# Seven products for eight in the last twelve f-tiles, and down tiles summed in DRAM

## The chip, the cores and the metric

The kernel runs on one core of a Trainium2 chip. A core has a matrix engine (TensorE, PE in the profile, with its weight loads shown apart as PEld), VectorE (DVE), ScalarE (ACT), GpSimd (POOL) and SyncE (SP), which here only issues DMAs. Each engine takes its instructions in the order in which they are written; between engines there are semaphores. The metric is the device time of one execution in microseconds, the median of several runs.

## What is computed

One layer norm of x (2048 tokens of 576) feeds two branches, whose results are added to x.

```
xn = layernorm(x)                                   # 2048 x 576
A:  q, k, v = xn @ wqkv;  32 heads of 18; each token attends to 8 earlier ones, 2 apart
    a = softmax(q.k / sqrt(18)) @ v;   A = a @ wo
B:  h  = gelu(layernorm(xn) @ w1);  quarters of h shifted by +1, -1, +2, -2 tokens
    x1 = xn + h @ w2
    B  = x1 + gelu(layernorm(x1) @ w3) @ w4          # w3: 576 x 4608, w4: 4608 x 576
out = x + A + B
```

All inputs and the output are 32-bit floats. The last line of B, the channel MLP with its up projection (w3) and its down projection (w4), is most of the work.

## The kernel before, in words

Products are computed with each operand split into a high part, which the matrix engine takes in its fast 32-bit format, and a low part, the rest. A product of 576 terms is 14 matmuls (`PAIRS`): high by high, high by low and low by high for four slices of 128 rows, and two for the last 64 rows, where high and low share a slice. A low part costs a copy on ACT (the high part) and a subtraction on DVE (`split_w`, L167 and L168, for weights, `split_x` for inputs).

The stages follow each other: q, k and v for 16 tiles of 128 tokens, spilled to DRAM (to about 195 us); the mixing MLP with w1 and w2 (to about 315 us); the channel MLP; the output projection with wo. The channel MLP runs in 72 units. A unit (`for u, (c, b) in enumerate(units)`) takes a pair of f-tiles, of 128 columns of w3 each, and one block of 512 tokens. Its order is:

- two up tiles (`up`, matmuls at L676): 14 matmuls of 512 columns each, gelu twice on ACT (L680 for the high part, L681 in full), the low part on DVE (L682);
- the four down tiles of the unit before (`down`, L696): 12 matmuls of 288 columns each into a PSUM buffer, then an addition to the running sum in `Y` on DVE (L699);
- a share of the weights: loads of w3 and w4 for later f-tiles on SP, their splits on ACT and DVE.

`Y` holds the sums of all 16 token tiles in SBUF for the whole stage. The token blocks come from `n_turn`: the normalised x1 is transposed on DVE, put to DRAM and fetched back in the other layout (`put`, `get`).

The attention (`attention`, a generator) runs on DVE in the gaps of the units: `bg(us)` lets it issue instructions for so many us between two pieces of a unit, by set costs (1.3 us for an operation of 1152 columns). `RATE` sets the amount per unit, 6.1 us. Its eight groups of four heads load q, k and v from DRAM and store their result in `od` (L614). Before the sixth unit from the end, `while not state["done"]` issues whatever is left. Then `load_o`, `o_turn` and `put` bring the attention's result into the layout that the output projection needs: 16 token tiles, loaded by SP (L738), transposed on DVE, put to DRAM by SP (L137) and fetched back. All loads and stores are issued by SP, in the written order; where one waits, those behind it wait.

Of the kernel before, what the change touches and what calls it, by code (L numbers as in the profile page):

```python
# [19 lines left out]
HD = 18  # L20
# [12 lines left out]


# [3 lines left out]
PAIRS += [(4, 4), (4, 9)]  # L38

# [6 lines left out]
def fused_block(ctx, tc, x, wqkv, wo, w1, w2, w3, w4, out):  # L46
# [8 lines left out]
    psa = ctx.enter_context(tc.tile_pool(name="psa", bufs=2, space=PSUM))  # L55
    psb = ctx.enter_context(tc.tile_pool(name="psb", bufs=3, space=PSUM))
# [10 lines left out]
    ST = RT = None  # L67
    xd = {}
    qkvd = dram.tile([24, HALO + S, GC], F32, name="qkvd")
    od = dram.tile([S, D], F32, name="od")  # L70
    bncnt = [0]
# [50 lines left out]
    def room(p):  # L122
        nonlocal ST, RT
        ST = p.tile([128, 20, 128], F32, name="st")
        RT = p.tile([128, 512], F32R, name="rt")
# [19 lines left out]
    def split_x(xt, part=None):  # L145
        raw = xt.bitcast(F32)
        if part != 1:
            act.copy(RT[64:128, :], raw[64:128, 4, :])
            act.copy(xt[0:64, 4, :], raw[0:64, 4, :])
            dve.tensor_tensor(xt[64:128, 4, :], raw[64:128, 4, :], RT[64:128, :].bitcast(F32),  # L150
                              op=ALU.subtract)
# [61 lines left out]
    def ring_block(key):  # L213
        if key not in xring:
            xring[key] = ring.tile([128, 9, 512], F32R, name="xt", tag="xt")
        return xring[key]
# [34 lines left out]
    pool.memset(low, 1.0)  # L251
    for g in range(4):
# [156 lines left out]
    rzp = tc.tile_pool(name="rzp", bufs=2, reuse_waits="tile")  # L409
    rzpool = rzp.__enter__()  # L410
# [3 lines left out]
    def load_w2(k):  # L414
        r = rzpool.tile([128, D], F32, name="rz", tag="rz")
# [80 lines left out]
    raws, W3, W4 = {}, {}, {}  # L496

    def load_f(f):
        if f >= NF:
            return  # L500
        r = raws[f] = wp.tile([128, 640 + D], F32, name="rawf", bufs=2)
        r3 = r[:, :640].rearrange("p (k c) -> p k c", k=5)
        main_rows(r3[:, 0:4, :], w3, f * 128, 128)
        dup_tail(r3[:, 4, :], w3, f * 128, 128)
        sp.dma_start(r[:, 640:], w4[f * 128:(f + 1) * 128, :])

    def split_w3(f):
        if f >= NF:
            return
        t = W3[f] = wp.tile([128, 10, 128], F32R, name="W3", bufs=3)  # L510
        split_w(t[:, 0:5, :], t[:, 5:10, :], raws[f][:, :640].rearrange("p (k c) -> p k c", k=5))

    def split_w4(f):
        if f >= NF:
            return
        t = W4[f] = wp.tile([128, 2, D], F32R, name="W4", bufs=3)
        split_w(t[:, 0, :], t[:, 1, :], raws[f][:, 640:])

    x1n = {}

    def n_turn(t, zpool):
        z = zpool.tile([128, D], F32, name="rz", tag="rz")
        act.activation(z, Y[:, t, :], AF.Identity, bias=RS[2][:, t, 0:1], scale=RS[2][:, t, 1:2])  # L523
        turn(z, t % 4)
        if t % 4 == 3:
            put(("n", t // 4))

    load_f(0)
    load_f(1)
    nsp = tc.tile_pool(name="nsp", bufs=1, reuse_waits="tile")  # L530
    room(nsp.__enter__())
    for t in range(NT):
# [12 lines left out]
        stats(Y[:, t, :], 2, t)  # L545
        if t in (1, 3):
            f = (t - 1) // 2
            split_w3(f)
            split_w4(f)
            load_f(f + 2)  # L550
        if 2 <= t < 6:
            n_turn(t - 2, rzpool)
        if t in (9, 10, 13, 14):
            k = {9: 4, 10: 6, 13: 8, 14: 10}[t]
            n_turn(k, rzpool)
            n_turn(k + 1, rzpool)
        if t in (8, 13):
            x1n[t // 13] = ring_block(("n", t // 13))
            get(("n", t // 13), x1n[t // 13])
        if t in (11, 15):  # L560
            split_x(x1n[t // 15])
    nsp.__exit__(None, None, None)
    rzp.__exit__(None, None, None)
    mp.__exit__(None, None, None)


    xp = ctx.enter_context(tc.tile_pool(name="xp", bufs=1, side="right", reuse_waits="tile"))
    for b in (2, 3):
        x1n[b] = xp.tile([128, 9, 512], F32R, name=f"x1n{b}")
    hp = ctx.enter_context(tc.tile_pool(name="hp", bufs=2, reuse_waits="tile"))  # L570
    tp = ctx.enter_context(tc.tile_pool(name="tp", bufs=1, reuse_waits="tile"))
    room(tp)
# [312 lines left out]
```

## Time and profile before

| | |
|---|---|
| median of 3 runs | 1294.08 us (1294.03 to 1295.88) |
| the profiled execution | 1294.73 us, span 1292.9 us |
| PE busy | 1285.0 us, 99% |
| DVE, ACT, POOL busy | 935.6, 362.0, 38.1 us |
| DMA | 125.20 MB, mean 97 GB/s |

The span is the profiled execution from its first to its last instruction; the time has some 2 us more around it. In the rows of instructions, the columns are line, engine, operation, output and inputs, shapes and count, then the busy time in us and the mean of one in ns. In timelines they are start, duration, engine, line and operation. In the rows by stretch each engine's busy time is followed by its number of instructions, and at the end stand the granted clock of PE, the busy share of the DMA engines and GB/s. In rows of DMAs the last number is the median time from issue to landing in us.

### The profile page before, as it was taken

To read this page: it belongs to the slowest core of one execution; us is meant where nothing else is said; L and a number is where in the kernel's file an instruction comes from. 1 tells how busy PE (TensorE), PEld (TensorE's weight loads), DVE (VectorE), ACT (ScalarE), POOL (GpSimd) and SP (SyncE) were. 2 spreads that over 40 slices of the span, in tenths; PEclk is the share of its full clock that TensorE was granted. 3 is DMA by queue.
4 is the path that set the end of the run, shared out by engine and by line. 5 is a ranking of instruction groups with operands and counts; after the bars stand their busy time and mean duration, and the time that the engine had idled before them with its cause. 6 is when DMAs were issued, how large, how long until landed. Compare 5 with 4: busy or idle time off the path is not lost.

```text
span 1292.9 us, 18505 instructions
## 1 busy us (share of the span) xinstructions
PE 1285.0 (99%) x7678; PEld 1184.8 (92%) x7678; DVE 935.6 (72%) x1336; ACT 362.0 (28%) x601; POOL 38.1 (3%) x108
## 2 busy tenths in 40 slices
PE   8999999999999999999999999999999999999998
PEld 8999998899899999989999999999998999999998
DVE  6455534689576778888878888878888878855741
ACT  3332126524412232232222132232232231213310
POOL 2011100021000000000000000000000000000000
PEclk9999999999999999999999999999999999999999
DMA  7646884346702030221221221221232111156842
GB/s 204 154 122 137 172 174 143 92 108 155 229 29 73 29 101 20 82 75 46 82 73 48 82 72 42 89 73 29 75 99 71 31 49 44 58 120 158 208 145 83
DMA packets 157828, 125.20 MB, mean 97 GB/s; under 512 B 72608, under 2 KB 129824, under 8 KB 157744
## 3 DMA queue, kind: packets, MB, share of 16 engines
q1 hardware_dynamic: 157744, 124.02, 34.9%
q8 instruction: 60, 0.98, 0.3%
q14 instruction: 24, 0.20, 0.0%
HBM read 83.56 MB, written 39.39 MB: 95 GB/s over the span
## 4 chain that ended last, share of the span: by engine, by line
PE 94%; DMA 2%; DVE 2%; ACT 1%; SPq 0%; issue 0%; ACTq 0%
PE ps L696 35%; PE p L676 34%; PE ps L182 17%; PE ps L431 4%; PE ps L276 3%; DMA xd<-st 1%; PE ps L446 1%; PE ps L104 1%; DMA xt<-xd 0%; DMA raw<-in_A_wqkv_dram 0%; DMA x1n<-xd 0%; DVE st L129 0%; SPq L137 0%; PE p L853 0%; ACT rz L523 0%
## 5 line engine op out<-in xcount | busy, mean ns | idle before, releaser
L696 PE MATMUL ps<-W,hi 128*128 128x288 f32 x2304 | 398.7, 294 | 0.5 <-DVE Y L699 0.4
L696 PEld LDWEIGHTS ps<-W,hi 128*128 128x128 f32 x2304 | 339.5, 188 | 7.2 <-DVE Y L699 1.0
L680 ACT ACTIVATE hi<-p 128x512 fp32r<-128x512 f32 x144 | 86.2, 598 | 578.4 <-PE p L676 578.4
L696 PE MATMUL ps<-W,lo 128*128 128x288 f32 x1152 | 245.3, 294 | 0.0
L676 PE MATMUL p<-x1n,W 128*128 128x512 f32 x1008 | 234.6, 389 | 0.0
L676 PE MATMUL p<-xt,W 128*128 128x512 f32 x1008 | 234.4, 389 | 0.0
L676 PEld LDWEIGHTS p<-xt,W 128*128 128x128 f32 x1008 | 187.3, 188 | 36.9
L676 PEld LDWEIGHTS p<-x1n,W 128*128 128x128 f32 x1008 | 187.3, 188 | 36.8
L699 DVE TENSOR_TENSOR Y<-ps,Y 128x576 f32<-128x576 f32 x288 | 212.0, 748 | 11.0 <-PE ps L696 10.7
L682 DVE TENSOR_TENSOR lo<-g,hi 128x512 fp32r<-128x512 f32 x144 | 99.5, 691 | 159.5 <-ACT g L681 159.4
L696 PEld LDWEIGHTS ps<-W,lo 128*128 128x128 f32 x1152 | 185.3, 187 | 0.0
L182 PE MATMUL ps<-WQ,xt 128*128 128x432 f32 x672 | 134.4, 359 | 0.0
L182 PEld LDWEIGHTS ps<-WQ,xt 128*128 128x128 f32 x672 | 125.5, 188 | 5.4
L628 DVE TENSOR_TENSOR prod<-q,k 128x1152 f32<-128x1152 f32 x64 | 86.4, 1349 | 0.0
L631 DVE TENSOR_REDUCE L<-prod 128x64 f32<-128x1152 f32 x64 | 86.1, 1346 | 0.0
L681 ACT ACTIVATE g<-p 128x512 f32<-128x512 f32 x144 | 85.3, 592 | 0.0
L612 DVE TENSOR_TENSOR o<-o,prod 128x1152 f32<-128x1152 f32 x56 | 75.5, 1349 | 0.0
L608 DVE TENSOR_TENSOR prod<-v,L 128x1152 f32<-128x1152 f32 x56 | 75.5, 1348 | 0.0
L167 ACT CAST W<-rawf 128x640 fp32r<-128x640 f32 x72 | 50.3, 700 | 70.5 <-PE ps L696 69.2
L168 DVE TENSOR_TENSOR W<-rawf,W 128x640 fp32r<-128x640 f32 x72 | 56.2, 783 | 0.0
L182 PE MATMUL ps<-W,h 128*128 128x288 f32 x384 | 53.5, 295 | 0.0
L182 PEld LDWEIGHTS ps<-W,h 128*128 128x128 f32 x384 | 51.9, 188 | 0.1
(108 smaller groups left out, 888.7 us busy)
## 6 DMA issues: line engine op xcount, KB each, us to landing
xd<-st SPq DMA_DIRECT2D x48, 320.0 KB, 6.0
qkvd<-stg SPq DMA_DIRECT2D x24, 432.0 KB, 3.6
rawf<-in_B_w_dram SPq DMA_DIRECT2D x36, 288.0 KB, 3.2
rawf<-in_B_w_dram SPq DMA_DIRECT2D x36, 256.0 KB, 3.0
xt<-xd SPq DMA_DIRECT2D x8, 768.0 KB, 5.1
xin<-in_A_x_dram SPq DMA_DIRECT2D x16, 288.0 KB, 3.8
q<-qkvd SPq DMA_DIRECT2D x8, 576.0 KB, 4.0
k<-qkvd SPq DMA_DIRECT2D x8, 576.0 KB, 5.0
```

Source lines behind the costliest of these rows:

```text
L168: dve.tensor_tensor(dst_lo, raw, dst_hi.bitcast(F32), op=ALU.subtract)
L182: pe.matmul(ps[:, h, :n], xs(a), ws(b, h), start=i == 0, stop=i == len(PAIRS) - 1)
L608: dve.tensor_tensor(dst, vv, Lf[:, :, w:w + 1].to_broadcast([128, TPP * GH, HD]), op=ALU.mult)
L612: dve.tensor_tensor(o, o, dst, op=ALU.add)
L628: dve.tensor_tensor(prod.rearrange("p (j h) d -> p j (h d)", h=GH), q, k[:, r0:r0 + TPP, :], op=ALU.mult)
L631: dve.tensor_reduce(Lf[:, :, w], prod, axis=AX.X, op=ALU.add)
L676: pe.matmul(ps, W3[f][:, w, :], x1n[b][:, a, :], start=n == 0, stop=n == len(PAIRS) - 1)
L680: act.activation(by_token(hi), in_order(ps), AF.Gelu_apprx_tanh)
L681: act.activation(by_token(g32), in_order(ps), AF.Gelu_apprx_tanh)
L682: dve.tensor_tensor(lo, g32, hi.bitcast(F32), op=ALU.subtract)
L696: pe.matmul(ps[:, k, :HF], h[:, col], w[:, p, k * HF:(k + 1) * HF], start=n == 0, stop=n == len(seq) - 1)
L699: dve.tensor_tensor(yv, ps[:, :, :HF], yv, op=ALU.add)
```

## The change

The first 12 pairs of f-tiles keep their units, 48 of them. The last 6 pairs (12 f-tiles) run in 12 steps `q`, six for the first 1024 tokens and six for the rest. A step multiplies a 2 x 2 scheme of blocks: the two halves of the 576 terms (288 each), the two f-tiles of the pair, and two blocks of 512 tokens. Instead of eight products of half length it forms seven, of sums and differences of the halves of w3 and of x1 (the scheme of Strassen and Winograd). A product of 288 terms is 7 matmuls (`HALVES`): six for two slices of 128 rows, and one for the last 32 rows, whose high and low parts share a slice.

- The sums of x1's halves are made in DRAM during the units, by accumulating DMAs from POOL (`sums`), and are fetched and split for the first 1024 tokens at the end of the units and for the others in step 5 (`get_op`, `split_op`; `swap`). Signs are put into the blocks when they are made (`n_turn`, `split_n`, `signed`).
- The sums of w3's halves are made in each step for the next one: `load_pair` fetches four blocks with 20 DMAs on SP, `combine` forms the sums on DVE, `split_a` and `split_s` make high and low parts on ACT and DVE.
- The products are added up on DVE (`z_add`) in four temporary tiles, and gelu is taken from these (`gelu_z`).
- Down tiles of 11 of the 16 token tiles (`YD`) are no longer added to `Y` by DVE: ACT copies the PSUM buffer to one of three temporary tiles, and POOL issues a DMA that adds it to a tile in DRAM (`yd`). 198 of the 288 down tiles go this way. At the end SP loads the eleven tiles back (`load_y`). The space of these tiles in `Y` serves as temporary storage and takes the raw w4.
- `RATE` becomes 8.0 us for a unit, 2.0 for the last two, 5.0 for a step, and 0.5 for steps 0, 5 and 6. What is left of the attention is issued before step 8 (`z == -4`). Behind it come `load_o`, `o_turn` and `put`, now one token tile at a time with two buffers, six in steps 8 and 9 each and four in step 10.

The PSUM buffers of the steps are four of 512 columns for products and two for down tiles. The new parts, cut:

```diff
+    def down(t, parts, pd):
...
+        if t in YD:
+            e = temp(EV[evc[0] % len(EV)], D)
+            evc[0] += 1
+            act.copy(e.rearrange("p (h c) -> p h c", h=2), ps[:, :, :HF])
+            pool.dma_start(yd[t], e, accum_op=ALU.add)
+        else:
             yv = Y[:, t, :].rearrange("p (h c) -> p h c", h=2)
             dve.tensor_tensor(yv, ps[:, :, :HF], yv, op=ALU.add)
...
+    def load_pair(q):
+        f = 2 * (NPL + q % NWP)
+        st = WS["st"] = wspool.tile([128, 4, 3, 128], F32, name="w3st")
+        for o, (g, k) in enumerate(((f, 0), (f, 1), (f + 1, 1), (f + 1, 0))):
+            r0, c0 = k * HF, g * 128
+            sp.dma_start(st[:, o, 1:3, :],
+                         w3[r0:r0 + 256, c0:c0 + 128].rearrange("(k p) c -> p k c", p=128))
+            for a in range(4):
+                sp.dma_start(st[32 * a:32 * a + 32, o, 0, :], w3[r0 + 256:r0 + HF, c0:c0 + 128])
...
+    def product(w, xk):
+        ps = pc.tile([128, 512], F32, name="cc", tag="c")
+        for i, (a, v) in enumerate(HALVES):
+            pe.matmul(ps, w[:, v, :], area[xk][:, a, :], start=i == 0, stop=i == len(HALVES) - 1)
+        return ps
...
+    def o_turn(t):
+        turn(otile[t], t % 4)
+        if t % 4 == 3:
+            put(("o", t // 4))
+        if t + 2 < NT:
+            load_o(t + 2)
...
+    ORDER = ["P1", "P2", "P6", "P5", "P7", "D0", "P4", "D1", "P3", "D2", "D3", "D4", "D5", "D6", "D7"]
+    for q in range(NQ):
...
+        if z == -4:
             while not state["done"]:
                 bg(1e9)
             open_wo()
+            for t in range(2):
+                load_o(t)
+        load_w4(p)
...
+        if z < -1:
+            load_pair(q + 1)
+        for it in (FIRST if q == 0 else SWAP if q == NWP else ORDER):
+            if it == "P1":
+                c1 = product(wv(a, "A11"), "B11")
+                act.copy(by_token(Z1), in_order(c1))
...
+            elif it == "P7":
+                c7 = product(wv(sw, "S3"), "T3")
+                z_add(Z3, c7, Z2)
+                z_add(Z1, c5, Z3)
+                z_add(Z2, c5, Z2)
+                low_part(h11, Z4)
+                if z < -1:
+                    split_a(q + 1, 0)
...
+            else:
+                j = int(it[1])
+                down(*prev[j], pd)
+                if j == 3:
+                    hid[q, "c22"] = gelu_z("c22", Z1)
+                    hid[q, "c12"] = gelu_z("c12", Z2)
+                if z < -1:
+                    if q and j == 2:
+                        combine()
+                    if q and j == 3:
+                        split_s(q + 1, 0)
+                    if j == (4 if q else 3):
+                        split_s(q + 1, 1)
...
+                if swap and j in (0, 2, 4, 6):
+                    split_op(("B11", "B21", "T2", "T1")[j // 2])
...
+            if z in (-4, -3, -2) and it in ("D2", "D3", "D4", "D5", "D6", "D7") and turned < NT:
+                o_turn(turned)
+                turned += 1
+            bg(r, it in ("D1", "D5"))
```

In these lines P is one of the seven products and D one of the eight down tiles of the step before; `z` counts steps from the end. Steps are counted from 0 here and in what follows, and D0 to D7 are their down tiles in order.

631 lines of the change are left out of this document (446 added, 185 removed).

## The prediction

> **What bounds the kernel now.** I read the page's header and busy shares first, then the chain of work in order of time, then the busy times by stretch.
>
> ```profile
> span 1292.9 us, 18505 instructions
> PE 1285.0 (99%) x7678; PEld 1184.8 (92%) x7678; DVE 935.6 (72%) x1336; ACT 362.0 (28%) x601; POOL 38.1 (3%) x108
> PEclk9999999999999999999999999999999999999999
> ...
> 448.24 6.36 PE p L676 x28
> 454.59 6.43 PE ps L696 x48
> 461.03 6.34 PE p L676 x28
> ...
> 380.00:1130.00 750.00, 750.00 (x4482) 684.38 (x4482) 618.67 (x713) 189.51 (x319) 0.00 (x0) 1.00 0.20 62
> ```
>
> PE is busy for 1285.0 of 1292.9 us and its clock is full in all slices. From 342 us on the chain is nothing but two pieces in turn: one unit's up projection, 28 matmuls of 512 columns in 6.36 us (227 ns each), and four down tiles, 48 matmuls of 288 columns in 6.34 us (132 ns each, 1.585 us a tile). A unit is 12.70 us. In the last row the columns are PE, PEld, DVE, ACT, POOL: over 750 us DVE has 618.67 (82%), so it hides behind PE with 18% to spare; ACT has 75%. The profiled execution took 1294.73 us (span 1292.9), the median of the three runs is 1294.08; my sum is made against 1294.7.
>
> **What is taken away.** A changed step does two units' work for one pair of f-tiles and two token blocks: 7 products of 7 matmuls, where two units had 56. That is 49 x 227 ns = 11.13 us and 8 down tiles of 1.585 us, 12.68: 23.8 us a step against 25.4. Twelve steps save 84 x 227 ns = 19.1 us. All other matmuls stay, so 1294.7 - 19.1 = 1275.6 us is the floor, if PE never waits more than before.
>
> **What is added, and the engines' rates.**
>
> ```profile
> 443.66 1.35 DVE L628 TENSOR_TENSOR prod<-q,k 128x1152 f32<-128x1152 f32 x1
> 444.93 0.75 DVE L699 TENSOR_TENSOR Y<-ps,Y 128x576 f32<-128x576 f32 x1
> ...
> 464.24 0.60 ACT L680 ACTIVATE hi<-p 128x512 fp32r<-128x512 f32 x1 [7.91 <-PE p L676]
> 464.73 0.59 ACT L681 ACTIVATE g<-p 128x512 f32<-128x512 f32 x1
> ...
> L154 ACT CAST xt<-xt 128x1024 fp32r<-128x1024 f32 x16 | 16.3, 1046 | 0.0
> ```
>
> Starts are closer than durations: 1.27 us for a 1152-column attention operation, 0.49 us for a 512-column activation. On DVE, 198 of the 288 down tiles' additions go (0.75 us each). A changed step puts back 7 additions of products, 4 low parts, 4 weight sums and the splits, some 15 us by these rates, beside 2 or 3 additions that stay and 5 us of attention: about 20 of 23.8 us. ACT gets 8 activations, 5 or 6 tile copies and 7 weight copies, about 12 us. Neither is the bound by its sum. What decides is order: both run strictly in the written order, so a tile's copy stands behind whatever its engine still waits for.
>
> The 198 tile additions become accumulating DMAs issued by POOL, 2.75 a unit, one per 4.6 us. The trace of before has no such DMA. From above: the slowest store, 320 KB, lands in 6.0 us, and one at a time this would be 1.4 us too slow for each of the 132 tiles that come from plain units, 182 us. From below: 288 KB stores land in 2.1 us, hidden; a gain is excluded, since no matmul goes with them. I take hidden, because each of the three buffers has about 11 us (a unit less one tile) before its reuse in the plain units, twice the slowest store, and three can be in flight.
>
> ```profile
> xd<-st SPq DMA_DIRECT2D x48, 320.0 KB, 6.0
> out_dram<-Y SPq DMA_DIRECT2D x15, 288.0 KB, 2.1
> ```
>
> **The SP queue.** Per changed step it gets 2 loads of W4 and 20 of W3 halves (four blocks, each one load of 128 rows and four of 32).
>
> ```profile
> 475.20 0.38 SPq L177 DMA_DIRECT2D rawf<-in_B_w_dram  x1
> 475.63 1.16 SPq L173 DMA_DIRECT2D rawf<-in_B_w_dram  x2
> 476.83 0.58 SPq L505 DMA_DIRECT2D rawf<-in_B_w_dram  x1
> ...
> 207.47 0.59 SPq L451 DMA_DIRECT2D v<-u  x1
> 208.11 0.58 SPq L452 DMA_DIRECT2D v<-u  x1
> ...
> rawf<-in_B_w_dram SPq DMA_DIRECT2D x72, 32.0 KB, 2.8
> ```
>
> A load of 128 rows holds SP 0.43 us with its gap, one of a few rows about 0.61 (207.47 to 208.11 is 0.64). A block is 0.43 + 4 x 0.61 = 2.87 us, the pair 11.5, with W4 12.5 us of 23.8; the last lands some 2.6 us after its issue. [...]
>
> Steps 1 to 4, 6 and 7: SP starts 1 to 2 us into a step, when DVE has split the last W4 (the W4 raw tiles are reused). Three blocks have landed at 2 + 1 + 8.6 + 2.6 = 14.2 us. ACT's copies of them (three, 1.4 us) stand in front of its copy of down tile D1, and D3 needs D1's PSUM buffer at 15.9 us (ten items of 1.59): just in time. After D3, ACT has one tile copy, four activations and three copies of the sums (4.4 us) before D5's (or, for the second token half, D4's) copy: 0.5 to 2 us late. I take 8 us for six steps, bounds 0 and 14. Step 0 has four tiles instead of eight to cover the same chain: 4 us (0 to 6).
>
> Step 5 also fetches the second half's seven operands: 35 loads, 7 x 2.87 = 20 us, behind the pair. The first lands at 1.5 + 12.5 + 2.9 + 2.6 = 19.5 us; its split (about 2.3 us on ACT, from the 1046 ns row and three smaller pieces) stands before D1's copy, so D3 starts near 22.5, not 15.9, and the other splits add 4 more: 10 us (6 to 13). The x1 blocks get a sign pass and stores ahead of the first units: 1 us (0 to 5).
>
> **Steps 8 to 10, where I expect the loss.** Before step 8 the kernel runs what is left of the attention in one go. The instruction order of the changed kernel shows how much: fourteen 1152-column operations on DVE with nothing between, 14 x 1.27 = 17.8 us, then the store of the last head group, then two tile loads of it, and only behind these, on the same SP queue, W4 and the pair for step 9.
>
> ```profile
> 1140.65 0.57 SPq L614 DMA_DIRECT2D od<-o  x1
> 1146.24 4.37 SPq L738 DMA_DIRECT2D ot<-od  x8
> 1175.41 4.15 SPq L137 DMA_DIRECT2D xd<-st  x4
> ...
> SPq L738 <- DMA od<-o: 4.9, 1, 4.9
> DMA to landing us min/median/max: 3.5/6.2/9.7
> ```
>
> The fourteen start when DVE has split W4, about 1.5 us into step 8, and end at 19.3. The loads follow the store's issue by 5.6 us (1140.65 to 1146.24, a wait for its landing): 24.9. Eight loads 4.4: 29.3; W4 1.0; three blocks 8.6: 38.9; landing 2.6: 41.5. ACT's three copies and D1's, 2.0: D3 starts at 43.5, not 15.9. That is 27.6 us. (The additions of the products wait in DVE too: the sixth product finds no free PSUM buffer from 9.5 to 21 us, inside the same wait.) Nothing hides it, since ACT takes its work in order.
>
> Then each step turns six attention tiles with two buffers, four loads a tile, on that same queue. From the landing of three blocks, L: the fourth L+2.9, sums L+4.7, first turn (0.9) L+5.6; its buffer's reload issues in 2.2, lands in 3.5 (the fastest of that row), turn L+12.2; again, L+18.8. The put of four turned tiles (4.2) lies before the next reload: the sixth turn ends at L+25.3, the seventh reload L+27.5, W4 28.4, three blocks 37.0, next landing L+39.6, where PE needs 23.8: 15.8 us lost in step 9. Step 10 has its put earlier, so L+43.9: 20.1 us. Six turns on DVE also hold the next step's first additions, inside these waits. The tail costs 27.6 + 15.8 + 20.1 = 63.5 us; with 0.43 us for every issue and every load landing in 2.6 us it is about 46; with that row's median landing of 6.2, 2.7 us more at each of three reloads in two steps and at the first loads, about 85. Step 11 and the loads of y at the end hide.
>
> Sum: 1294.7 - 19.1 + 63.5 + 10 + 4 + 8 + 1 = 1362 us.
>
> The clock is 1.00 in every stretch of this trace, which has no long wait of PE, so the cost of cooling down cannot be read here. [...]
>
> **Rivals.** First, only the flush costs and the reload loop does not chain (the buffers reload earlier than I laid out): 1362 - 35.9 = 1326. For it: with shorter landings the loop nears 23.8; against: SP alone has 35 us of issue in steps 8 and 9 each. Chance 0.17. Second, the accumulating DMAs run one at a time and bound the plain units: 1362 + up to 182, some 1450 if they take 5.3 us each. For it: nothing in the trace shows their price; against: the DMA engines are 20% busy in the long row above. Chance 0.07. Third, on the other side: issuing costs SP almost nothing, and everything of the pair lands 2.6 us after its turn. Its place is the SP queue behind the flush; D3 of step 8 then starts at 19.3 + 5.6 + 2.6 + 2.0 = 29.5, 13.6 late, the loop takes some 15 us and hides, steps 0 to 7 lose 2: 1294.7 - 19.1 + 15.6 = 1291. It decides below about 0.05 us an issue; the rows have 0.4 to 0.6. Chance 0.09. My forecast holds 0.67.
>
> **Numbers.** 1362 us. Low end: the tail at 46 and the earlier losses at a third, 1294.7 - 19.1 + 46 + 8 = 1330; the first rival with its earlier losses at a third would be 1311, and I stop between, at 1318. High end: the tail at 85 and the rest as summed is 1384, with the earlier terms at their upper bounds 1399; I stop at 1395. The second and third rivals stay outside. Within 0.2% (2.6 us, about what three runs can tell) I give 0.02, faster 0.07, slower 0.91.
>
> **What would show it.** Right: matmul count 7594; three steps of the last stage longer than 38 us, with PE idle before a down tile and ACT as its releaser, ACT idle for the DMA of the W3 blocks, SP without gaps for tens of us; fourteen attention operations back to back on DVE; one step in the middle about 34 us; plain units still at 12.7 us. Wrong: SP's issues shorter than 0.4 us, D3 of the ninth step on time, or plain units longer than 12.7 us with ACT waiting for POOL's DMAs.

## The result, and the profile after

The changed kernel takes 1418.2 us (median of four runs, 1416.7 to 1418.6) against 1294.2: 1.095 times the time before (95% interval 1.093 to 1.097), slower, and 23 us above the range that was given. The profiled execution has a span of 1416.9 us. From its page, the header, the busy times and the clock in 40 slices:

```profile
span 1416.9 us, 20066 instructions
PE 1309.4 (92%) x7594; PEld 1197.8 (85%) x7594; DVE 955.5 (67%) x1315; ACT 585.8 (41%) x937; POOL 227.7 (16%) x329
PEclk9999999999999999999999999999998997888899
```

These three lines hold the whole account. PE has 84 matmuls fewer and yet is busy 24.4 us longer. At the speed of before it would be busy 1285.0 - 19.1 = 1265.9 us, so 43.5 us are matmuls that take longer than before, and six of the last ten slices of the clock show 7 or 8 where all stood at 9. PE idles 107.5 us against 7.9. The span grew by 124.0 = -19.1 (products saved) + 43.5 (slow matmuls) + 99.6 (waits).

Most of the 43.5 us is the clock. In this trace it stands either at 1.00 or at 0.50, at 0.50 in 16 pieces of 3.41 to 10.24 us. The sum of these pieces, and of PE's busy time in them:

```profile
sum 102.43, PE 70.24; mean PE 4.39
```

From the start of seven matmuls of 512 columns to that of the next ones it is 3.14 us at 0.50 (1179.09 to 1182.23 us) and 1.61 at 1.00 (1183.81 to 1185.42), nearly twice. Taken as twice, an estimate, 70.2 us of matmuls at 0.50 are 35.1 us more than at 1.00. The other 8.4 us then come at full clock, as the 1.0 us of steps 2 to 4 in the table below; what makes them was not tried.

Where the waits and the slow matmuls lie is read from the busy times by stretch; the stretches are the plain units, then steps 0, 1, 2 to 4, 5, 6, 7, 8, 9, 10, 11 with the last eight downs, and the output projection. After the length stand PE, PEld, DVE, ACT and POOL, then the granted clock, the DMA share and GB/s.

```profile
342.00:914.00 572.00, 561.73 (x3344) 511.43 (x3343) 440.07 (x445) 227.42 (x365) 123.76 (x141) 0.99 0.78 162
935.22:953.17 17.95, 17.85 (x99) 15.45 (x98) 17.51 (x24) 14.22 (x22) 2.57 (x3) 1.00 0.42 82
953.17:985.52 32.35, 26.91 (x148) 22.94 (x146) 24.46 (x36) 19.38 (x30) 4.45 (x6) 0.95 0.52 97
985.52:1061.26 75.74, 72.42 (x438) 65.74 (x436) 63.59 (x83) 42.42 (x66) 13.03 (x15) 1.00 0.61 114
1061.26:1098.98 37.72, 28.30 (x148) 25.61 (x146) 26.30 (x36) 23.59 (x36) 4.37 (x5) 0.84 0.82 205
1098.98:1128.01 29.03, 25.86 (x146) 22.25 (x146) 25.90 (x36) 23.18 (x35) 4.39 (x5) 0.98 0.55 122
1128.01:1158.40 30.39, 26.72 (x147) 24.48 (x146) 22.51 (x31) 14.03 (x22) 5.21 (x6) 0.89 0.78 165
1158.40:1209.37 50.97, 28.64 (x147) 25.57 (x146) 35.02 (x43) 13.70 (x22) 5.29 (x6) 0.80 0.43 92
1209.37:1250.99 41.62, 30.25 (x148) 27.19 (x146) 17.74 (x29) 13.70 (x22) 5.29 (x6) 0.84 0.73 164
1250.99:1298.88 47.89, 30.73 (x148) 26.87 (x146) 24.19 (x42) 13.81 (x22) 5.27 (x6) 0.79 0.67 152
1298.88:1353.86 54.98, 45.10 (x243) 41.26 (x242) 28.44 (x35) 30.05 (x45) 10.43 (x12) 0.84 0.93 248
1353.86:1416.90 63.04, 59.42 (x450) 59.18 (x448) 12.28 (x17) 0.64 (x1) 0.88 (x1) 1.00 0.34 111
```

A step needs 23.8 us of PE at full speed. Length less PE busy is waiting, PE busy less 23.8 is what slow matmuls cost (step 0 has four downs, 17.5 us; the stretch of step 11 needs 36.5):

| step | length | waiting | slow matmuls | predicted loss |
|---|---|---|---|---|
| before step 0 | | 13.3 | 2.5 | 1 |
| 0 | 18.0 | 0.1 | 0.4 | 4 |
| 1 | 32.4 | 5.4 | 3.1 | |
| 2 to 4 | 75.7 | 3.3 | 1.0 | 1 to 4, 6, 7: 8 |
| 6, 7 | 59.4 | 6.8 | 5.0 | |
| 5 | 37.7 | 9.4 | 4.5 | 10 |
| 8 | 51.0 | 22.3 | 4.8 | 27.6 |
| 9 | 41.6 | 11.4 | 6.5 | 15.8 |
| 10 | 47.9 | 17.2 | 6.9 | 20.1 |
| 11 and last downs | 55.0 | 9.9 | 8.6 | 0 |

Hardly a step gains. The quietest, 2 to 4, take 25.25 us, nearly the 25.4 us of two units: of the 1.6 us that a step saves, 0.2 is left. The waits of PE, from the timeline of the changed kernel (start, duration, then in brackets the wait before and what ended it):

```profile
353.20 3.18 PE L799 MATMUL ps<-w,c 128*128 128x288 f32 x12 [6.50 <-ACT Y L804]
1009.07 1.86 PE L799 MATMUL ps<-w,c 128*128 128x288 f32 x12 [1.11 <-ACT Y L804]
1179.09 3.30 PE L998 MATMUL cc<-xt,w3a 128*128 128x512 f32 x7 [10.97 <-DVE Y L1002]
1197.00 7.57 PE L799 MATMUL ps<-w,c 128*128 128x288 f32 x36 [9.83 <-ACT Y L804]
1246.18 4.97 PE L799 MATMUL ps<-w,c 128*128 128x288 f32 x24 [2.67 <-ACT Y L804]
1319.41 6.13 PE L799 MATMUL ps<-w,c 128*128 128x288 f32 x24 [2.86 <-ACT Y L804]
1333.08 5.65 PE L799 MATMUL ps<-w,c 128*128 128x288 f32 x22 [1.53 <-DVE w L561]
```

Two things are to be seen. Most waits end with ACT's copy of a down tile (L804), as forecast. And the matmuls behind a long wait are slow: twelve of a down tile take 3.18 us behind 6.50 us of waiting and 1.86 behind 1.11.

Ahead of step 0 the timeline of ACT shows what the prediction had at 1 us:

```profile
349.44 0.63 ACT L595 ACTIVATE Y<-x1n 64x512 fp32r<-64x512 f32 x1 [6.44 <-DMA x1n<-xn]
438.59 0.64 ACT L804 COPY Y<-ps 128x576 f32<-128x576 f32 x1 [8.33 <-DMA yd<-Y]
```

In the third unit ACT waits for a token block to split, with three tiles' copies behind it; before the change DVE took these tiles out. At 438 us POOL stands for 9.3 us at the sums in DRAM, each of which waits for the one before, and the tile DMAs behind it free their buffers late.

### The profile page after: what moved, and what is told of

The parts are those of the page before. It is cut to its first block, busy times and chain, and to the rows that moved or that the text cites. A ratio compares the mean times of both kernels' runs of the same rounds, so it can differ in the third digit from the quotient of the medians.

```text
span 1416.9 us, 20066 instructions
## 1 busy us (share of the span) xinstructions
PE 1309.4 (92%) x7594; PEld 1197.8 (85%) x7594; DVE 955.5 (67%) x1315; ACT 585.8 (41%) x937; POOL 227.7 (16%) x329
## 3 DMA queue, kind: packets, MB, share of 16 engines
q0 software_dynamic: 32528, 66.37, 30.8%
## 4 chain that ended last, share of the span: by engine, by line
PE 44%; issue 18%; DMA 4%; ACT 3%; POOL 3%; DVE 2%; SPq 1%; POOLq 0%; ACTq 0%; DVEq 0%
PE ps L799 19%; PE p L786 17%; PE cc L998 4%; PE ps L212 4%; POOL yd L805 3%; DMA yd<-Y 2%; DMA w3st<-in_B_w_dram 1%; ACT Y L804 1%; SPq L879 1%; DMA x1n<-td1T 1%; ACT c L775 0%; ACT w3s L891 0%; DMA xt<-td1T 0%; DMA Y<-in_B_w_dram 0%; DMA x1n<-xn 0%
## 5 line engine op out<-in xcount | busy, mean ns | idle before, releaser
L799 PE MATMUL ps<-w,c 128*128 128x288 f32 x3456 | 503.9, 305 | 75.7 <-ACT Y L804 67.8
L799 PEld LDWEIGHTS ps<-w,c 128*128 128x128 f32 x3456 | 492.1, 197 | 90.2 <-ACT Y L804 73.8
L805 POOL DMA_DIRECT2D yd<-Y x198 | 174.4, 905 | 789.4 <-ACT Y L804 756.5
L804 ACT COPY Y<-ps 128x576 f32<-128x576 f32 x198 | 125.2, 638 | 234.8 <-PE ps L799 158.1
L780 DVE TENSOR_TENSOR c<-Y,c 128x512 fp32r<-128x512 f32 x144 | 98.9, 687 | 103.7 <-ACT Y L770 100.2
L769 ACT ACTIVATE c<-p 128x512 fp32r<-128x512 f32 x96 | 57.4, 598 | 157.6 <-PE p L786 157.6
L786 PE MATMUL p<-xt,w3a 128*128 128x512 f32 x336 | 78.9, 391 | 1.6 <-ACT Y L770 1.6
L786 PE MATMUL p<-x1n,w3s 128*128 128x512 f32 x336 | 78.6, 390 | 0.0
L786 PE MATMUL p<-xt,w3s 128*128 128x512 f32 x336 | 78.5, 390 | 0.0
L786 PE MATMUL p<-x1n,w3a 128*128 128x512 f32 x336 | 78.5, 390 | 0.0
L704 DVE TENSOR_TENSOR o<-o,prod 128x1152 f32<-128x1152 f32 x56 | 75.7, 1352 | 0.6
L786 PEld LDWEIGHTS p<-x1n,w3a 128*128 128x128 f32 x336 | 62.5, 188 | 12.6
L786 PEld LDWEIGHTS p<-x1n,w3s 128*128 128x128 f32 x336 | 62.4, 188 | 12.6
L786 PEld LDWEIGHTS p<-xt,w3s 128*128 128x128 f32 x336 | 62.4, 188 | 12.6
L808 DVE TENSOR_TENSOR Y<-ps,Y 128x576 f32<-128x576 f32 x90 | 67.4, 749 | 8.5 <-PE ps L799 8.3
L119 POOL TENSOR_TENSOR rs<-rs,mhalf 128x1 f32<-128x1 f32 x48 | 30.4, 633 | 255.1 <-DVE rs L118 148.0
```

Source lines behind the costliest of these rows:

```text
L704: dve.tensor_tensor(o, o, dst, op=ALU.add)
L769: act.activation(by_token(h[:, 0, :]), in_order(ps), AF.Gelu_apprx_tanh)
L780: dve.tensor_tensor(h[:, 1, :], g, h[:, 0, :].bitcast(F32), op=ALU.subtract)
L786: pe.matmul(ps, W3[f][:, w, :], x1n[b][:, a, :], start=n == 0, stop=n == len(PAIRS) - 1)
L799: pe.matmul(ps[:, k, :HF], h[:, col], w[:, p, k * HF:(k + 1) * HF], start=n == 0, stop=n == len(seq) - 1)
L804: act.copy(e.rearrange("p (h c) -> p h c", h=2), ps[:, :, :HF])
```

## The experiments

Sixteen kernels ran, with one time and one profile each; the kernel before took 1294.2 to 1294.8 us beside them. e1 and e13 are the same up to step 8 and begin step 0 at 938.5 and 943.1 us, so differences of less than some 5 us in that column, or in a total, are not read. Lengths are differences of the starts of the first product of each step, in us; the last one ends with the first matmul of the output projection.

| run | time | step 0 at | 0 and 1 | 2, 3, 4 | 5 | 6 | 7 | 8 | 9 | 10 | 11, last |
|---|---|---|---|---|---|---|---|---|---|---|---|
| PE at full speed | | | 41.3 | 23.8 each | 23.8 | 23.8 | 23.8 | 23.8 | 23.8 | 23.8 | 36.5 |
| changed | 1418.2 | 935.2 | 50.3 | 25.3 each | 37.7 | 29.0 | 30.4 | 51.0 | 41.6 | 47.9 | 55.0 |
| e1 attention done | 1393.0 | 938.5 | 48.9 | 25.3, 25.3, 25.4 | 36.8 | 28.8 | 26.8 | 26.8 | 40.3 | 48.9 | 56.5 |
| e2 weights first | 1411.3 | 938.9 | 50.5 | 25.3, 25.3, 25.5 | 38.2 | 29.4 | 27.9 | 42.0 | 38.7 | 50.3 | 54.5 |
| e3 merged loads | 1438.8 | 935.7 | 50.9 | 25.3 each | 36.9 | 36.0 | 29.5 | 55.1 | 43.6 | 54.8 | 56.0 |
| e4 early part | 1408.1 | 925.1 | 50.8 | 25.3 each | 36.9 | 30.8 | 29.2 | 50.6 | 41.2 | 47.2 | 55.7 |
| e5 turns spread | 1406.2 | 938.4 | 67.5 | 25.3, 34.4, 25.9 | 45.1 | 28.3 | 28.4 | 28.1 | 36.5 | 28.2 | 55.2 |
| e6 and pairs sooner | 1385.2 | 938.5 | 65.5 | 25.2, 28.4, 25.2 | 44.2 | 29.1 | 26.8 | 28.1 | 26.8 | 26.8 | 55.7 |
| e7 and the end | 1380.0 | 938.3 | 65.6 | 25.2, 26.8, 25.2 | 44.1 | 29.4 | 28.1 | 26.8 | 26.8 | 30.5 | 48.2 |
| e8 merged od loads | 1441.9 | 936.5 | 50.4 | 25.2, 25.2, 26.1 | 37.4 | 28.9 | 29.5 | 54.3 | 48.2 | 55.3 | 60.2 |
| e9 mended | 1373.0 | 934.8 | 52.6 | 25.3, 38.1, 25.3 | 39.0 | 27.7 | 28.4 | 28.7 | 28.3 | 30.9 | 49.3 |
| e10 copies on DVE | 1402.7 | 936.5 | 52.7 | 29.6, 38.4, 29.0 | 33.9 | 29.1 | 28.4 | 41.3 | 29.3 | 42.2 | 47.6 |
| e11 no accumulation | 1365.5 | 932.4 | 48.6 | 25.3 each | 34.9 | 29.1 | 28.2 | 26.8 | 36.7 | 42.4 | 45.8 |
| e12 short copies | 1384.6 | 937.1 | 47.1 | 24.3 each | 35.3 | 30.9 | 27.5 | 25.9 | 37.9 | 49.7 | 55.4 |
| e13 doubled od issues | 1415.7 | 943.1 | 48.7 | 25.3 each | 36.6 | 30.2 | 26.8 | 26.8 | 46.9 | 58.5 | 57.4 |
| e16 pair in 12 loads | 1380.5 | 935.0 | 47.2 | 25.3 each | 33.1 | 29.2 | 28.1 | 26.8 | 40.2 | 47.5 | 52.5 |
| e17 order | 1348.4 | 931.0 | 48.8 | 25.3 each | 36.4 | 33.1 | 26.8 | 28.2 | 26.8 | 26.8 | 49.9 |

### The flush before step 8 (e1, e2)

```diff
-    RATE = [8.0, 2.0, 5.0, 0.5]
+    RATE = [9.0, 2.0, 5.0, 0.5]          # e1
```
```diff
-        if z == -4: (flush, open_wo, load_o)
         load_w4(p)
...
             load_pair(q + 1)
+        if z == -4: (flush, open_wo, load_o)      # e2
```

> The one edit: the background attention is fed 9.0 us of vector work per plain unit in place of 8.0, so that nothing of it is left when step 8 begins. Theory 1 (vector queue): the 14 attention operations flushed in front of step 8, and the store, od loads and weight loads behind them on SP, are what makes step 8 51.0 us long; without them it is 27 to 33 us (23.8 us of products and downs, plus the od and weight loads that remain on SP), and the time is 1418 less 18 to 24, so 1394 to 1400 us. Theory 2 (transfers): step 8 is late because the chip moves too many bytes in it; then it stays at 45 us or more, and the time is above 1412 us. The plain units stay at 12.7 us by both.

> The one edit: in step 8 the loads of W4 and of the next weight pair go onto the SP queue ahead of the attention flush, the od store and the first od loads; the flush stays. Theory 1a (SP order is what counts): D3 no longer waits for weights, step 8 is below 35 us, time 1398 to 1404 us. Theory 1b (the flush on VectorE counts by itself, since the sums of step 8's products queue behind 14 operations of 1.39 us): step 8 still loses most of those 19 us, is 43 to 49 us, time 1408 to 1416 us. Theory 2 (transfers): no change, 1416 to 1420 us.

Without the flush step 8 falls from 51.0 to 26.8 us, and PE's clock in it rises from 0.80 to 1.00 with the same products in it; the time falls by 25 us. With the flush left in and only SP's order changed, step 8 is still 42.0: some 15 of the 24 us stay with the flush, and PE's long wait in it, 11.82 us, ends with DVE's addition of a product; the other 9 are the weights' place behind it. In e1 steps 9 and 10 stay long, and SP's timeline shows why: step 9 begins at 1182.5 us, and the weights for step 10 go out behind a put and twelve od loads.

```profile
1184.38 6.16 SPq L166 DMA_DIRECT2D xd<-st  x4
1190.58 8.74 SPq L1032 DMA_DIRECT2D ot<-od  x12
1199.42 0.84 SPq L553 DMA_DIRECT2D Y<-in_B_w_dram  x2
```

### Does the number of issues hold SP? (e3, e8, e13, e16)

```diff
-            for a in range(4):
-                sp.dma_start(st[32 * a:32 * a + 32, o, 0, :], w3[r0 + 256:r0 + HF, c0:c0 + 128])
+            sp.dma_start(st[:, o, 0, :], dram_ap(w3, (r0 + 256) * n3 + c0, [[0, 4], [n3, 32], [1, 128]]))
...                                         # e3; the same in get_op and load_o; e8: load_o alone
```
```diff
-        for q in range(4):
-            sp.dma_start(otile[t][32 * q:32 * q + 32], dram_ap(od, ..., [[D, 32], [1, D]]))
+        for q in range(8):
+            sp.dma_start(otile[t][16 * q:16 * q + 16], dram_ap(od, ..., [[D, 16], [1, D]]))     # e13, on e1
```
```diff
+            if o in (1, 3):                                                             # e16, on e1
+                two = slice(1, 3) if o == 1 else slice(0, 4, 3)
+                rows = w3[r0 + 256:r0 + HF, f * 128:f * 128 + 256]
+                for a in range(4):
+                    sp.dma_start(st[32 * a:32 * a + 32, two, 0, :], rows.rearrange("p (o c) -> p o c", o=2))
```

> The one edit: the four 32-row loads of each weight block, operand block and od tile become one DMA each with the same bytes, so a weight pair is 8 issues in place of 20, an operand 2 in place of 5, an od tile 1 in place of 4. Theory 1 (SP issue): at 0.475 us an issue every step's weights land 5.7 us sooner; steps 1, 6 and 7 lose 3 to 5 us less each, steps 5, 8, 9 and 10 lose 4 to 10 us less each: 25 to 45 us in all, time 1373 to 1393 us. Theory 2 (the transfers themselves or the landing are late, the issues are not): at most 8 us less, time 1410 to 1419 us.

> The changed kernel with one edit: an od tile is loaded by one DMA of 128 rows in place of four of 32; no load that repeats rows is touched. It tells which part of the third run's edit made steps 6, 8 and 10 longer. If the repeated rows of the weight and operand loads are what is slow as one DMA, steps 9 and 10 are now 2 to 8 us shorter than the changed kernel's 41.6 and 47.9 us and steps 0 to 7 as they were, time 1405 to 1416 us. If any merged DMA is slower, steps 9 and 10 are 2 to 7 us longer, time 1422 to 1430 us.

Both came out slower than either theory allowed. The timelines of SP for the same operand of step 5 (its load of 128 rows and its repeated rows), in the changed kernel and in e3, and one more merged load of e3:

```profile
1087.37 0.54 SPq L848 DMA_DIRECT2D x1n<-td1T  x1
1088.01 3.30 SPq L850 DMA_DIRECT2D x1n<-td1T  x4
```
```profile
1080.97 1.21 SPq L848 DMA_DIRECT2D x1n<-td1T  x1
1082.27 6.25 SPq L850 DMA_DIRECT2D x1n<-td1T  x1
...
1072.94 0.55 SPq L850 DMA_DIRECT2D x1n<-xn  x1
```

One merged DMA holds SP 6.25 us where its four parts took 3.30, another of the same size 0.55, so a row of SP is not only the price of issuing. All seven operands hold SP 28.0 us in e3 with 14 issues, and 23.4 in the changed kernel with 35. The merged loads have a dimension of four outermost, where each of the parts had its 32 rows; why they hold SP longer was not shown. So e3 and e8 changed the transfer with the number, and don't settle the question.

> The first run's kernel with each od tile loaded by eight DMAs of 16 rows in place of four of 32, the same bytes: 24 issues more in each of steps 8 and 9. If SP's queue is held by the number of issues (0.475 us each), the weights behind them come 8 to 11 us later and steps 9 and 10 are 46 to 60 us long in place of 40.3 and 48.9: time 1405 to 1415 us. If it is held by the bytes in front, as the third and eighth runs suggest (fewer issues, not sooner), steps 9 and 10 stay within 3 us: time 1385 to 1397 us.

> The first run's kernel with a weight pair loaded by 12 DMAs in place of 20: the 32-row pieces of two blocks that lie side by side in w3 go as one, each still with its 32 rows outermost, the same bytes. [...] If issues hold the queue (0.475 us each), the weights land 3.8 us sooner, steps 9 and 10 are 3 to 4.5 us shorter each and steps 1, 6 and 7 up to 2: time 1380 to 1387 us. If transfers do, all steps stay within 1.5 us and the time within 4 us of 1393.

With the same bytes in twice as many od loads, steps 9 and 10 grow by 6.6 and 9.6 us; 24 issues take 12.83 us, 0.53 each.

```profile
1180.37 12.83 SPq L1032 DMA_DIRECT2D ot<-od  x24
```

Issues do hold the queue in the reload loop. In e16 the pair has eight issues fewer and the total falls by 12.6 us, as foretold, but not where: steps 9 and 10 lose 0.1 and 1.4 us less, not 3 to 4.5, step 5 3.7 and the end 4.0, and 3.5 of the rest lie ahead of step 0, where only the first pair's loads differ and e1 and e13 differ by 4.6 without any. That the pair's own issues cost steps 1 to 4, 6, 7, 9 and 10 what the prediction said is not shown.

### The part before step 0 (e4)

```diff
-        if 5 <= u < 13: sums((u - 5) // 4, (u - 5) % 4)
+        if u in SUMS: sums(*SUMS[u])       # units 6, 8, 11, 14 and 16, 18, 21, 24
...
-            if u in (1, 2) and i == 0: split_n(u + 1, x1n[u + 1], 0, RT)
+            if u in (1, 2) and j in (1, 2): split_n(u + 1, x1n[u + 1], j - 1, RT)     # behind downs
...                                         # load_w3p, load_w4 of unit 0 go to unit 1
```

> Two edits ahead of the plain units' steady run: the DRAM sums on GpSimd's queue are issued two or three units apart in place of one, and in the first units ScalarE splits the next token block only after it has copied out two more down tiles, with the weight loads moved behind the block's load on SP. Theory 1 (in-order queues: copies behind a split that waits for its load, tile DMAs behind a sum that waits for another sum): the 6.5 us wait in front of unit 3 falls to 0 to 3 us and the waits of 2.4 and 1.4 us at 446 and 486 us go; 7 to 11 us less, time 1407 to 1411 us. Theory 2 (the accumulating DMAs take bandwidth in these places whatever the order): the waits stay or move, time within 3 us of 1418.

Step 0 begins 10.1 us sooner and the time falls by 10.1. The waits of 6.50, 2.39 and 1.38 us are gone; from the third unit on at most 0.8 is left in any place. It was the order on ACT and on POOL.

### Steps 9 and 10, and the end (e5, e6, e7, e9, e10)

```diff
-            if z in (-4, -3, -2) and it in ("D2", "D3", "D4", "D5", "D6", "D7") and turned < NT:
+            if q in (1, 2, 3, 4, 7, 8, 9, 10) and it in ("D3", "D7") and turned < NT:      # e5
                 o_turn(turned)
...
                         split_s(q + 1, 1)
+                        if z < -2: load_pair(q + 2)                                        # e6
...
-                if z == -1 and j in (0, 1, 5, 6, 7): split_wo(...)
+                if z == -2 and j in (1, 2, 5, 6, 7): split_wo(...)                         # e7
...
+                down(*prev[j], pd, dve if j in (5, 7) else None)                           # e10
```

> Three edits: the early mends of the fourth run, attention at 8.5 us a unit so that it ends before step 0, and the 16 turns of the attention output (its od loads, transposes and stores) two to a step in steps 1 to 4 and 7 to 10, in place of 16 in steps 8 to 10. Theory 1 (the weights of steps 9 and 10 stand on SP behind od loads and stores that wait, so their place is the cause): steps 9 and 10 fall from 40.3 and 48.9 us in the first run to 26 to 29 us each; with 10 us from the early part the time is 1340 to 1355 us. Theory 2 (the loads' own bytes and vector work cost wherever they stand): the 16 turns cost steps 1 to 4 and 7 to 10 some 30 us together, time 1370 us or more.

> The fifth run, and each weight pair is loaded right behind the last split that frees its staging buffer, in the step before, in place of the start of the next step. Theory 1 (the distance from load to use is what steps 5, 6 and 7 lack): step 5 has its SP queue free for the operand loads 10 us sooner and falls from 37 us to 28 to 32, steps 6 and 7 lose at most 2 us each; time 10 to 18 us below the fifth run. Theory 2 (step 5 is bound by the bytes of the seven operand loads, 5.4 MB in 23 us, whichever comes first): step 5 stays at 35 us or more and step 6 takes up what is gained, time within 5 us of the fifth run.

> The sixth run, with the turns in steps 1 to 4 and 6 to 9, the output weights split in step 10 in place of step 11, and the first two blocks of the attention output split two downs later in step 11. Theory 1 (in step 11 ScalarE holds tile copies behind splits that wait for loads): step 11 with the last downs falls from 55 us to 40 to 45 us, with PE's clock back at 1.00 in it; time 10 to 15 us below the sixth run. Theory 2 (the end is bound by transfers, 243 to 298 GB/s, and by a clock that the loads of PE set): 50 us or more, and the clock stays below 0.9.

These three have a fault: at 8.5 us a unit the attention was not done, and its last store stood on SP inside step 0 (at 960.8 us), which makes steps 0 and 1 some 17 us longer. So e5 takes 1406.2 us, far above the 1340 to 1355 expected. Apart from the fault, e5 frees steps 8 and 10 and puts waits into steps 3, 5 and 9, wherever the fourth turn's put stands in front of weights. e6 takes the weights out of that queue and steps 7 to 10 are 26.8 to 28.1 us each: their loss was the place of the weights behind the turns. Step 5 does not gain (44.2): now the next pair, a put and four od loads stand in front of its operands, which go out from 20 us into the step. e7 shortens the end by 7.5 us, to 48.2 and not to the 40 to 45 expected, and lengthens step 10 by 3.7.

> The seventh run with its own fault mended: attention is fed at 9.0 us a unit as in the first run, so that no flush is left (at 8.5 its last store stood on SP at 960.8 us, inside step 0, with the weight pair behind it), the operands of step 0 are fetched half a unit to a unit sooner, the turns stand in steps 1 to 3 and 7 to 9 so that step 5's loads find SP free, and step 1 puts two downs ahead of the products that need the late weights. If each wait is one of order on SP or ScalarE, as the theory says: steps begin at 921 to 927 us, steps 0 and 1 together 43 to 47 us, step 5 28 to 36 us, the others 25 to 27 us, step 11 with the last downs 44 to 48 us, granted clock above 0.98: time 1318 to 1340 us. If the work itself binds (ScalarE 13.9 us a step and the operand splits of steps 5 and 6 on top; a clock set by load), steps 5 and 6 stay at 66 us or more together and the time is 1345 us or more.

> The ninth run, and in the steps two of the copies of down tiles go to VectorE (downs 5 and 7), with one more buffer for copied tiles. It tests what holds the quiet steps 2 to 4 at 25.25 us where 13 products and downs need 23.8: if it is the copies' place behind the activations on ScalarE (waits of 0.4 and 1.1 us in each step), these steps fall to 23.8 to 24.4 us and the time is 8 to 14 us below the ninth run; if it is the landing of the accumulating DMAs (three buffers, 5 to 6 us each) or PE itself, they stay at 25 us or more and the time is within 4 us.

e9 missed its 1318 to 1340 us. Its turns were now 6 us apart, and in step 3 one waits for the put of the four before; the additions of the products stand behind it on DVE. The row of DVE in e9, then the one of PE:

```profile
1030.92 0.71 DVE L158 STREAM_TRANSPOSE st<-ot 128x512 f32<-128x512 f32 x1 [15.80 <-DMA xd<-st]
```
```profile
1033.05 3.36 PE L1004 MATMUL cc<-xt,w3a 128*128 128x512 f32 x7 [10.68 <-DVE Y L1008]
```

In e10 copies went to DVE and came behind such turns: 30 us worse. Its od tiles also have one buffer where e9 has two, so it tells nothing on ACT's copies, and e12 was made for that.

### What the second half of the change costs (e11, e12)

```diff
-            pool.dma_start(yd[t], e, accum_op=ALU.add)                     # e11, on e1
```
```diff
-            act.copy(e.rearrange("p (h c) -> p h c", h=2), ps[:, :, :HF])
+            act.copy(e.rearrange("p (h c) -> p h c", h=2)[:, :, :16], ps[:, :, :16])     # e12, on e1
```

> The first run's kernel (attention done before step 8) without the 198 accumulating DMAs of the down tiles: the tiles are still copied out of PSUM, but not added up in DRAM, so 57 MB less move and a copy's buffer is free at once; the output lacks these sums. It measures what the second half of the change costs. Theory 1 (the order on the in-order queues is the cause, the accumulating DMAs are nearly hidden): only the waits of copies for a buffer go; steps 2 to 4 stay at 25.2 us, steps 5, 9, 10 and the end lose 1 to 3 us each less, time 1378 to 1390 us. Theory 2 (these DMAs crowd the operand, od and weight loads): steps 5, 9, 10 and the end are 5 to 10 us shorter each, time 1350 to 1372 us.

> The first run's kernel with each copy of a down tile on ScalarE cut to 32 of its 576 columns, in its place in the queue and with the same DMA behind it; the sums of the other columns are left out, so the output lacks them. Theory 1 (a copy is late because of what stands ahead of it on ScalarE, not because of its 638 ns): PE's waits on the copies shrink by the half microsecond that a copy is shorter, steps 2 to 4 go from 25.25 to 24.4 to 25.0 us, steps 9 and 10 stay at 39 us or more, time 1375 to 1388 us. Theory 2 (ScalarE's load is what binds): steps 2 to 4 fall to 23.8 to 24.2 us, steps 5 and 6 by 5 us each and the end by 8 us or more, time 1345 to 1370 us.

The accumulating DMAs cost 27.6 us in e1, not the few that I expected: 10.7 at the end, 6.5 and 3.6 in steps 10 and 9, 1.9 in step 5, and 6.1 ahead of step 0, little more than two executions can differ there. In the plain units they are hidden, as predicted; it is where od, operands, Wo and y are loaded too that they tell. e11 takes away both their traffic and ACT's waits for a free copy buffer (29.8 us of ACT in e1), and does not tell the two apart. The copies' own length is worth 0.9 us in a quiet step: the last wait of steps 2 to 4 in e12,

```profile
1006.84 1.85 PE L799 MATMUL ps<-w,c 128*128 128x288 f32 x12 [0.20 <-ACT Y L804]
```

against 1.11 us in the changed kernel. ACT is busy 56% of these steps (42.42 of 75.74 us). What stands in front of the copy is seen in its timeline at the end of step 1 of the changed kernel:

```profile
978.00 0.64 ACT L804 COPY Y<-ps 128x576 f32<-128x576 f32 x1 [1.41 <-PE ps L799]
978.53 0.63 ACT L775 ACTIVATE c<-Y 128x512 fp32r<-128x512 f32 x1
...
980.92 1.03 ACT L891 CAST w3s<-w3st 128x1024 fp32r<-128x1024 f32 x1
...
983.14 0.63 ACT L804 COPY Y<-ps 128x576 f32<-128x576 f32 x1
```

Four activations and three copies of weights lie between two tiles' copies, 5.1 us, while PE makes a down tile in 1.6. The longest waits stay in e12: 11.80 us in step 10 and 6.24 in step 5, against 12.73 and 6.46 in e1.

### What a wait costs beside its length (e15)

```diff
         hi = hp.tile([128, 512], F32R, name=f"hi{i}")
...
+        for _ in range(EXTRA.get(4 * c + b, 0) * i):        # in the kernel before
+            act.activation(by_token(hi), in_order(ps), AF.Gelu_apprx_tanh)
```

> The kernel before, with ten waits of known place: in every fourth unit from the 13th to the 49th, 4, 6, 7, 8, 10, 12, 16, 24, 32 and 48 repeats of one activation on ScalarE (0.49 us each) ahead of the one that the next down tile needs, so PE waits some 1 to 23 us, with the same results. It measures what a wait costs PE beside its own length, in a kernel that holds full clock. If the low clock of the steps comes from PE's idling, the waits longer than about 2.7 us are each followed by matmuls at half speed that cost 1.3 to 3 us more, the short ones by none; the waits sum to 70 to 80 us, so the time is 1294 + 70 to 80 + 9 to 20, 1373 to 1394 us. If the low clock comes from the products or their load, the clock stays at 1.00 here, the matmuls behind the waits keep 0.132 us each, and the time is the waits' sum alone, 1364 to 1374 us.

The time was 1406.6 us, above the 1373 to 1394 expected, because the waits sum to 93.3 us and not to 70 to 80. Busy times, waits of PE on down tiles, and three places of the timeline of this run:

```profile
PE 1304.6 (93%) x7678; PEld 1200.3 (85%) x7678; DVE 935.8 (67%) x1336; ACT 461.9 (33%) x768; POOL 38.1 (3%) x108
```
```profile
PE ps L699 <- DVE Y L702: 93.3, 11, 29.3
```
```profile
472.94 0.80 PE L699 MATMUL ps<-W,hi 128*128 128x288 f32 x4 [0.94 <-DVE Y L702]
583.26 1.33 PE L699 MATMUL ps<-W,hi 128*128 128x288 f32 x4 [3.55 <-DVE Y L702]
...
887.32 1.33 PE L699 MATMUL ps<-W,hi 128*128 128x288 f32 x4 [14.19 <-DVE Y L702]
```

The same 7678 matmuls take 1304.6 - 1285.0 = 19.6 us more, in a kernel whose clock was 1.00 throughout. Nine of the waits are 2.87 us or longer: 2.2 us each on average, and no more behind 14.19 us than behind 3.55; four matmuls take 1.33 us behind them and 0.80 behind a wait of 0.94. So PE's own idling lowers the clock, not the products: this kernel has none of them, and its granted clock is 1.00 up to the end of the wait of 3.55 us (560.00 to 583.20 us) and 0.76 in the 6.50 us behind it (583.26 to 589.76). Waits down to 2.87 us were already enough here: behind the one of 2.87 us eight matmuls of 512 columns take 3.34 us, 417 ns each against 227.

The granted clock of the changed kernel also shows why a short wait can cost as much, and waits in a row more. Its pieces at 0.50 are all one, two or three times 3.41 us long, as if the clock were set anew every 3.41 us. Seven stretches of that length in step 11 (start and end, length, PE's busy time, then the clock, the DMA share and GB/s):

```profile
1315.32:1318.73 3.41, 1.23 (x10) 1.00 1.08 339
1318.73:1322.15 3.42, 2.74 (x11) 0.50 1.05 378
1322.15:1325.56 3.41, 3.39 (x15) 0.50 1.08 327
1325.56:1328.97 3.41, 2.90 (x20) 1.00 1.07 293
1328.97:1332.38 3.41, 1.33 (x9) 1.00 1.10 296
1332.38:1335.80 3.42, 2.72 (x11) 0.50 1.07 261
1335.80:1339.21 3.41, 2.93 (x13) 0.50 0.44 155
```

Behind a stretch in which PE is busy for 1.23 or 1.33 us the clock is 0.50. It is 1.00 again behind 3.39 and 2.93 us, but not yet behind 2.74 and 2.72. From 346 us on, with all stretches cut at these boundaries, the clock fell sixteen times, each time behind 1.60 us of busy time or less; it never fell behind 1.85 or more, and one of 1.55 left it at 1.00. So short waits can do it together: in the fifth stretch a wait of 1.25 us and the first half of one of 1.53 us add up, and the rest of the latter keeps the clock low for a second stretch. Where a wait falls counts too: of four waits of 2.68 us in steps 7 to 10 of e17, three have 24 matmuls in 3.44 us behind them, and one (to 1175.42 us) has them in 4.77.

### All mends of order (e17)

The edits of e4, e6, e7 and e16, attention at 9.0, operands of step 0 fetched sooner, and

```diff
+            if q in (1, 2, 3, 4, 6, 7, 8, 9) and it in ("D0", "D6") and turned < NT:
                 o_turn(turned)
...
+        if q in (0, 6):                     # load_o(0), load_o(1); load_o(8), load_o(9) only here
```

> All mends of order together, so that each shows without the others' faults: early part as in the fourth run, attention at 9.0 us a unit, pairs loaded a step sooner and by 12 DMAs, the turns of the attention output 12.7 us apart in steps 1 to 4 and 6 to 9 with the ninth and tenth tile's load put off to step 6, output weights split in step 10. If what is lost is order, no step but the fifth, sixth and the end is above 27 us and the time is 1325 to 1350 us, still above the kernel before, since the quiet steps (25.25 us) save 0.2 us each against two units. If the work of the steps itself overloads ScalarE, VectorE or the DMA engines, waits come up elsewhere and the time is 1360 us or more, as in the ninth run.

1348.4 us, 70 less than the changed kernel with the same products, copies and accumulating DMAs. PE is busy 1285.1 us, so the slow matmuls cost 19.2 instead of 43.5 us, and it idles 61.5 instead of 107.5. Steps 7 to 10 are 26.8 to 28.2 us each. The time is in the range expected, but steps 1 and 8, with 31.2 and 28.2 us, are above the 27 us expected of them. What remains is 54 us above the kernel before: no kernel here beats it.

## Why the prediction was wrong

The direction and the place were right, the size was not: 1362 us forecast, 1418 measured. Against the sum, term by term:

- **Saved products, 19.1 us.** Right by count (7594 matmuls, plain units 12.7 us).
- **The clock, which "cannot be read here" and stood at nothing in the sum.** This is the step that failed: slow matmuls cost 43.5 us, 35.1 of them by the granted clock, as estimated above. Without it the forecast's 86.5 us of losses stand against 99.6 us of waits, within 13 us. That this is so near is partly luck: steps 8 to 10 waited 12.6 us less than forecast, the part ahead of step 0 and step 11 waited 12.3 and 9.9 more. e15 measures 2.2 us at a wait that stands alone; the changed kernel has nine of 2.8 us or more, some 20 us. Much of the rest comes behind shorter waits: 24 matmuls take 4.97 us behind 2.67 us, and 22 take 5.65 behind 1.53, against some 3.2 and 2.9 at 132 ns each. The stretches shown with e15 say how: short waits add up within one stretch of 3.41 us, and the next ones delay the return to full clock.
- **Steps 8 to 10, 63.5 us.** The mechanism was right: D3 of step 8 began 38.6 us into it, forecast 43.5; fourteen attention operations stood back to back, the od store at 1177.9 us, the weights behind the od loads. e1 and e6 take the two causes away one by one and steps 8 to 10 fall to 26.8 to 28.1. Their lengths lose 69.1 us, but 50.9 of that is waiting and 18.2 slow matmuls: the waits were too long in the forecast (a pair's block held SP 2.37 us, not 2.87), and the clock made up for it, by luck.
- **Step 5, 10 us.** 9.4 us of waiting, and 4.5 of slow matmuls. The mechanism was right: D3 began 22.8 us into it, forecast 22.5, behind the split of the first operand on ACT.
- **Steps 0 to 4, 6 and 7, 12 us.** 15.7 us of waiting in all, but not by the chain that was laid out: step 0 lost nothing, and in steps 2 to 4 the wait is at the last down tile, behind activations on ACT, not at D3 behind the loads. What holds steps 1, 6 and 7 was only seen in part.
- **Ahead of the first units, 1 us.** 13.3 us of waiting. Mis-sized because I looked at the sign pass and not at what stood behind it: e4 shows that it is copies behind a split that waits for its load, and tile DMAs behind sums.
- **"Step 11 and the loads of y at the end hide."** They don't: 9.9 us of waiting and 8.6 of slow matmuls. e11 and e7 take 10.7 and 7.5 us off, without the accumulating DMAs and by another order.
- **The accumulating DMAs, taken as hidden.** Right for the plain units, wrong for the steps, 27.6 us by e11.

Of the rivals, the third (issuing costs nothing) is out: e13 and step 8's queue show the issues. The first is out, since the reload loop did chain; the second too, with plain units at 12.7 us.

## What to carry to other kernels

Sum a change's waits first, and then add the clock that they cost PE: 2.2 us on average in e15 behind each wait of 2.87 us or more, and as much in the changed kernel behind shorter ones that together left PE idle for some 2 of 3.41 us. The kernel before, at 99% of PE, had this to lose as well as the waits: 19.6 us beside 93.3 in e15. When work moves from one in-order engine to another (tiles taken out by ACT instead of DVE, sums on POOL), go through everything that will stand in front of it in the new queue, wherever that engine waits for a load. And compare a quiet step with the quiet unit that it replaces before anything else: 25.25 against 25.4 us says that even with all order mended little could have come of it.

## What the hardware showed that was not expected

- Waits of 2.87 to 29.29 us cost PE 2.2 us on average beside their length, where the clock had been 1.00; 0.94 us cost nothing. The granted clock was 0.50 or 1.00 and changed in pieces of 3.41 us; it fell behind a stretch with 1.33 us of busy time, stayed low behind 2.74 and rose behind 2.93.
- Loads merged from four into one, with the four outermost, held SP for 0.55 to 6.25 us each, and made steps longer by up to 7 us.
- An accumulating DMA of 288 KB holds POOL 0.91 us and lands in 5.2 us; nearly hidden in the plain units (DMA share 0.78), but worth 10.7 us in the stretch with a share of 0.93.
- Kernels that are the same up to step 8 reached step 0 at 938.5 and 943.1 us.
